# Moving eight record scatters of GpSimd from the attention phase into the first dense steps

## The chip, the cores and the metric

The program runs on one core of a Trainium2 chip. The metric is the time of one execution on the device in microseconds (us). The engines are TensorE (PE; PEld is its weight load), VectorE (DVE), ScalarE (ACT), GpSimd (POOL) and SyncE (SP), which here only issues transfers.

## The reference

Sigmoid attention is followed by a mixture of experts in which each token goes to one expert.

```python
# q, k, v: [8 batches, 12 heads, 448 tokens, 64]
scores = q @ k.T / sqrt(64) - log(448)
attn_out = sigmoid(scores) @ v
x = attn_out.transpose(0, 2, 1, 3).reshape(3584, 768)
logits = x @ w_gate                       # [3584, 8]
expert_idx = argmax(logits, axis=1)
gate_w = softmax(logits)[arange, expert_idx]
for e in range(8):
    mask = expert_idx == e
    out[mask] = gate_w[mask, None] * (relu(x[mask] @ w1[e]) @ w2[e])   # w1[e]: 768x1024, w2[e]: 1024x768
```

## The kernel before

**Two parts in one stream.** The whole order is written by hand. `attention()` is a generator over steps s. A step is one chunk of 64 keys for two pairs of heads: `scores` (L616), sigmoid on ScalarE (L602), `weighted` (L632). There are 168 such steps, 21 for each batch (`PB`). Below step `START` = 70 the steps hold attention alone, two steps at a time. From step 70 on (the dense part), TensorE mostly runs expert matmuls: the caller runs seven of them each time that `attention()` yields (`MIX` is (7, 7), so fourteen a step), and every seventh step holds a burst of seven attention steps.

**The dense expert work.** `moe(b, wts)` runs the 448 tokens of one batch through one expert, the one that most of that batch's tokens chose. A w1 block j (eight for a batch) is 18 matmuls (L240) into one of two PSUM buffers (`ps`), then a relu on ScalarE that gives the high part `hh` (L247), and a VectorE operation that gives the low part `hl` (L248) and frees the PSUM buffer. Then come three output blocks d of twice 24 matmuls (L263) with w2.

**Weights in two parts.** A weight tile is loaded by SyncE's queue into `wst` (five buffers), split by ScalarE into a high part (L159) and by GpSimd, which subtracts the high part from the raw tile, into a low part (L160): a w1 part is 128x768, a w2 part 128x512. `Weights.ahead(n)` issues these splits. A w1 block calls it at its start with 3, 4, 5, 6, 7, 9, 11 and 13 parts for blocks 0 to 7 (the first eight parts are w1, then twelve w2); in an output block it is called after every second group of three matmuls of the second half, for one part more each time. The first three w1 parts are split before step 70.

**Where each token goes.** After attention for a batch b, stages named by letters are issued at fixed steps: "b", "c", "c2", "c3" work out the choice of expert and the gates, "d" (`gate_d`) ends by writing `si`, the four columns of slot indices of that batch (L403), a tile with two buffers. Stages "s0" to "s3" (`gate_d2`) write the batch's records (token number and gate, eight bytes) into the list `recs` in DRAM, one column of 112 tokens at a time, with an indirect transfer on GpSimd's queue (L424). "s0" first fills the token numbers on GpSimd (L413) and copies the gates on VectorE (L416). Nothing reads `recs` before the dense part is over; then the tokens that didn't go to their batch's expert are gathered by it.

**What sets the order around the change.** `PLACES` maps a step to its stages. A place r of batch b stands at step (b + 1) * 21 + r; below step 70 an odd one is moved up by one. So the first batch's scatters stand at steps 34, 36, 38 and 40, the second's at 56, 58, 60 and 62. In the dense part a step's stages stand between its two groups of seven matmuls. "d" of batch 2 stands at step 78. During attention's own phase GpSimd's queue also issues K loads (L545) and V loads (L558, L562) of the first 22 pairs; in the dense part those are on SyncE's queue.

Of the kernel before, what the change touches and what calls it, by code (L numbers as in the profile page):

```python
# [24 lines left out]
def tile_sigmoid_attention_top1_moe(  # L25
# [632 lines left out]
    START = 70  # L658
# [3 lines left out]
    PB = NP // 2 * ST  # L662
# [10 lines left out]
    def attention():  # L673
# [53 lines left out]

        LATE = {8: "b", 10: "c", 11: ("l", "c2"), 12: "c3", 15: "d", 16: "g", 26: "e"}
        FOUR = ("s0", "s1", "s2", "s3")
        PUTS = 2 * (dict(zip((13, 15, 17, 19), FOUR)),) + 4 * (dict(zip((27, 28, 29, 30), FOUR)),)  # L730
        PUTS += (dict(zip((25, 26, 27, 28), FOUR)), {9: "s0", 10: "s1"})
        LAST = {3: "b", 5: "c", 6: ("l", "c2"), 7: "c3", 8: "d", 9: "g"}
        EARLY = {5: "b", 7: ("c", "c2"), 9: ("l", "c3"), 11: "d", 13: "g", 32: "e"}
# [2 lines left out]
        for b in range(B):  # L736
            places = (EARLY, EARLY, FIRST_LATE, LATE, LATE, LATE, LATE, LAST)[b]
            for r, what in [*places.items(), *PUTS[b].items()]:
                at = (b + 1) * PB + r
# [20 lines left out]
        for s in range(N_ST + 11):  # L760
# [19 lines left out]
            if s >= START:  # L780
                b, r = divmod(s - 3 * PB, PB)
# [35 lines left out]
    for s, n in attention():  # L817
        if s >= START:
            more(n)
# [362 lines left out]
```

## Time and profile before

| | us |
|---|---|
| median of 3 runs (lowest to highest) | 776.97 (776.0 to 777.6) |
| the profiled execution, own time | 776.84 |
| its span, first to last instruction | 775.0 |
| TensorE matmul busy | 768.4 |
| TensorE weight load busy | 593.3 |
| VectorE busy | 373.9 |
| ScalarE busy | 384.1 |
| GpSimd busy | 349.6 |

The granted clock of TensorE is 1.000 over the span. Busy times are unions of what ran on an engine; the end of a matmul is modelled, so the start times of matmuls tell more than their ends. In rows of a timeline the columns are the start and the duration in us, engine, line, operation, output<-inputs, shapes and count; what stands in brackets is the idle time of the engine before it and what ended it.

### The profile page before, as it was taken

How to read it: one execution, taken by the hardware profiler on the slowest of the kernel's cores; microseconds unless marked ns; L12 is line 12 of the kernel's file. 1: busy time of each engine (PE TensorE's matmuls, PEld its weight loads, DVE VectorE, ACT ScalarE, POOL GpSimd, SP SyncE). 2: the span in 40 equal slices, each digit the busy share in tenths (PEclk: the TensorE clock that was granted, in tenths of full speed). 3: DMA queues.
4: the chain of work that ended last, by engine and by line, in shares of the span. 5: the costliest groups of instructions: out<-in, count | busy, mean ns of one | idle time of the engine just before them, and what ended most of it. 6: DMA issues, size and time to landing. Idle time of an engine off the chain costs nothing. (4 is left out here: it accounts for less than half of the span.)

```text
span 775.0 us, 15532 instructions
## 1 busy us (share of the span) xinstructions
PE 768.4 (99%) x5586; PEld 593.3 (77%) x5586; DVE 373.9 (48%) x806; ACT 384.1 (50%) x688; POOL 349.6 (45%) x330
## 2 busy tenths in 40 slices
PE   9999999999999999999999999999999999999997
PEld 6555557687696786867868769677698999999996
DVE  2354584465264652537426384254736493244543
ACT  5877776645536455264443653545523342444451
POOL 8648554242352342531615316054265764664351
PEclk9999999999999999999999999999999999999999
DMA  9777798976758846587585876766167554655770
GB/s 207 169 160 157 171 251 197 210 171 154 169 129 173 201 107 166 139 190 168 116 194 84 193 169 144 183 168 166 38 171 170 157 146 118 202 143 155 220 223 38
DMA packets 311633, 125.67 MB, mean 162 GB/s; under 512 B 210062, under 2 KB 307006, under 8 KB 311552
## 3 DMA queue, kind: packets, MB, share of 16 engines
q1 hardware_dynamic: 305504, 112.42, 61.9%
q0 software_dynamic: 5760, 11.76, 5.4%
q8 instruction: 45, 0.74, 0.4%
q10 hardware_dynamic: 288, 0.46, 0.2%
q14 instruction: 36, 0.29, 0.1%
HBM read 102.49 MB, written 22.49 MB: 161 GB/s over the span
## 5 line engine op out<-in xcount | busy, mean ns | idle before, releaser
L602 ACT ACTIVATE at<-sc,bias_s 128x448 f32<-128x448 f32 x336 | 192.3, 633 | 107.4 <-PE sc L616 106.5
L160 POOL TENSOR_TENSOR w1l<-wst,w1h 128x768 fp32r<-128x768 f32 x72 | 132.7, 1853 | 173.9 <-ACT w1h L159 172.2
L160 POOL TENSOR_TENSOR w2l<-wst,w2h 128x512 fp32r<-128x512 f32 x84 | 107.0, 1298 | 138.7 <-ACT w2h L159 121.0
L616 PE MATMUL sc<-qt,kt 64*64 64x448 f32 x1344 | 167.3, 545 | 0.0
L632 PE MATMUL av<-at,vn 64*64 64x448 f32 x1344 | 165.0, 536 | 0.0
L240 PE MATMUL ps<-xh,w1h 128*128 128x448 f32 x336 | 124.4, 370 | 0.2 <-DVE nw L439 0.2
L240 PE MATMUL ps<-xh,w1l 128*128 128x448 f32 x336 | 123.4, 367 | 0.0
L240 PE MATMUL ps<-xl,w1h 128*128 128x448 f32 x336 | 123.3, 367 | 0.0
L263 PE MATMUL ps<-hh,w2l 128*128 128x448 f32 x336 | 123.3, 367 | 0.0
L263 PE MATMUL ps<-hl,w2h 128*128 128x448 f32 x336 | 123.2, 367 | 0.0
L263 PE MATMUL ps<-hh,w2h 128*128 128x448 f32 x336 | 122.7, 365 | 0.0
L616 PEld LDWEIGHTS sc<-qt,kt 64*64 64x64 f32 x1344 | 78.2, 189 | 56.9 <-issue 44.4
L632 PEld LDWEIGHTS av<-at,vn 64*64 64x64 f32 x1344 | 59.4, 133 | 64.3 <-issue 53.5
L159 ACT CAST w2h<-wst 128x512 fp32r<-128x512 f32 x108 | 64.7, 620 | 75.7 <-PE ps L263 64.5
L247 ACT ACTIVATE hh<-ps 128x448 fp32r<-128x448 f32 x56 | 30.6, 546 | 139.6 <-PE ps L240 137.0
L276 DVE TENSOR_TENSOR ps<-ps,gt 128x448 f32<-128x448 f32 x42 | 40.7, 969 | 85.4 <-PE ps L263 85.3
L495 DVE STREAM_TRANSPOSE xt<-av 128x448 f32<-128x448 f32 x46 | 27.3, 629 | 101.5 <-PE av L632 100.4
L248 DVE SCALAR_TENSOR_TENSOR hl<-ps,hh 128x448 fp32r<-128x448 f32 x56 | 34.4, 614 | 78.3 <-ACT hh L247 76.8
L240 PEld LDWEIGHTS ps<-xh,w1h 128*128 128x128 f32 x336 | 63.1, 188 | 9.9 <-issue 4.4
L263 PEld LDWEIGHTS ps<-hh,w2l 128*128 128x128 f32 x336 | 65.2, 194 | 6.6 <-issue 3.5
L263 PEld LDWEIGHTS ps<-hl,w2h 128*128 128x128 f32 x336 | 65.2, 194 | 6.2 <-issue 3.2
L263 PEld LDWEIGHTS ps<-hh,w2h 128*128 128x128 f32 x336 | 65.2, 194 | 3.4 <-DVE nw L439 0.2
(158 smaller groups left out, 918.9 us busy)
## 6 DMA issues: line engine op xcount, KB each, us to landing
wst<-in_moe_w_dram SPq DMA_DIRECT2D x72, 384.0 KB, 3.3
wst<-in_moe_w_dram SPq DMA_DIRECT2D x54, 512.0 KB, 5.1
x_tok<-xt SPq DMA_DIRECT2D x64, 168.0 KB, 2.8
qn<-in_q_dram SPq DMA_DIRECT2D x184, 56.0 KB, 3.1
raw<-x_tok SPq DMA_DIRECT2D x28, 336.0 KB, 6.2
out_dram<-ob SPq DMA_DIRECT2D x84, 112.0 KB, 2.4
kn<-in_k_dram SPq DMA_DIRECT2D x104, 56.0 KB, 3.3
kn<-in_k_dram POOLq DMA_DIRECT2D x80, 56.0 KB, 4.0
```

What stands on the lines that cost most here:

```text
L159: nc.scalar.copy(hi, st)
L160: eng.tensor_tensor(lo, st, hi.bitcast(F32), op=ALU.subtract)
L240: nc.tensor.matmul(ps[:, :S], a[:, ws], b_, start=(t == 0 and n == 0), stop=(t == KD - 1 and n == 2))
L247: nc.scalar.activation(hh[:, :S], ps[:, :S], AF.Relu)
L248: nc.vector.scalar_tensor_tensor(hl[:, :S], ps[:, :S], 0.0, hh[:, :S].bitcast(F32), op0=ALU.max, op1=ALU.subtract)
L263: nc.tensor.matmul(ps[:, :S], a, b_, start=(j == 0 and n == 0), stop=(j == KF - 1 and n == 2))
L276: nc.vector.tensor_tensor(by_gate, by_gate, gate_rows[b], op=ALU.mult)
L495: nc.vector.transpose(xts[b][:, :, t, :], pv[:, :S].rearrange("p (j s) -> p j s", s=32))
L602: nc.scalar.activation(at, ps[:, :S], AF.Sigmoid, bias=bias_s, scale=SCALE)
L616: nc.tensor.matmul(ps[quarter(g, h), :S], ks, ops[g, "q"][OWN[h]], start=True, stop=True)
L632: nc.tensor.matmul(psv[g][OWN[h], :S], ops[g, "v"][rows, c, :], at[rows], start=(c == 0), stop=(c == KC - 1))
```

## The change

Only the places of the scatters of the first two batches differ. The new tuple gives the first batch the steps 70, 72, 74 and 76 (`START - PB` is 49, and 21 is added back), the second the steps 80, 82, 84 and 86. The fills and copies of "s0" move with them. The other six batches keep their places. The number of instructions is the same.

```diff
         FOUR = ("s0", "s1", "s2", "s3")
-        PUTS = 2 * (dict(zip((13, 15, 17, 19), FOUR)),) + 4 * (dict(zip((27, 28, 29, 30), FOUR)),)
+        PUTS = tuple(dict(zip(range(r, r + 8, 2), FOUR)) for r in (START - PB, START + 10 - 2 * PB)) + 4 * (dict(zip((27, 28, 29, 30), FOUR)),)
         PUTS += (dict(zip((25, 26, 27, 28), FOUR)), {9: "s0", 10: "s1"})
```

## Rows read from the trace of the kernel before

**Rows 1.** The page's first part: busy us (share of span) and count.

```profile
PE 768.4 (99%) x5586; PEld 593.3 (77%) x5586; DVE 373.9 (48%) x806; ACT 384.1 (50%) x688; POOL 349.6 (45%) x330
```

**Rows 2.** TensorE's waits, whole span: us in total, times, longest.

```profile
PE ps L240 <- DVE nw L439: 0.2, 1, 0.2
```

**Rows 3.** Timeline of TensorE in attention's own phase.

```profile
14.56 1.66 PE L616 MATMUL sc<-qt,kt 64*64 64x448 f32 x12
...
29.59 1.66 PE L616 MATMUL sc<-qt,kt 64*64 64x448 f32 x12
...
61.71 2.02 PE L632 MATMUL av<-at,vn 64*64 64x448 f32 x16
...
73.73 2.02 PE L632 MATMUL av<-at,vn 64*64 64x448 f32 x16
```

**Rows 4.** Line 424, all 32 scatters: duration in ns, who waited, landing.

```profile
L424 POOL DMA_INDIRECT recs<-rec,si x32: 941/958/1045, 63.0 to 609.6; - x32
...
  POOL kn L545: 0.4, 1
...
DMA to landing us min/median/max: 2.6/3.2/7.5
```

**Rows 5.** Timeline of GpSimd in attention's own phase: a scatter.

```profile
111.47 0.96 POOL L424 DMA_INDIRECT recs<-rec,si  x1 [0.30 <-issue]
```

**Rows 6.** Timeline of GpSimd, 131 to 198 us.

```profile
131.09 1.84 POOL L160 TENSOR_TENSOR w1l<-wst,w1h 128x768 fp32r<-128x768 f32 x1 [5.13 <-ACT w1h L159]
...
158.94 1.29 POOL L160 TENSOR_TENSOR w2l<-wst,w2h 128x512 fp32r<-128x512 f32 x1
160.63 2.56 POOL L160 TENSOR_TENSOR w2l<-wst,w2h 128x512 fp32r<-128x512 f32 x2 [0.40 <-ACT w2h L159]
164.48 2.55 POOL L160 TENSOR_TENSOR w2l<-wst,w2h 128x512 fp32r<-128x512 f32 x2 [1.28 <-ACT w2h L159]
184.61 5.06 POOL L160 TENSOR_TENSOR w2l<-wst,w2h 128x512 fp32r<-128x512 f32 x4 [17.58 <-DMA x_tok<-xt]
194.37 3.80 POOL L160 TENSOR_TENSOR w2l<-wst,w2h 128x512 fp32r<-128x512 f32 x3 [4.70 <-ACT w2h L159]
```

**Rows 7.** Timeline of VectorE, 163 to 165 us.

```profile
163.72 0.17 DVE L403 TENSOR_SCALAR si<-sl 112x4 uint32<-112x4 f32 x1
163.90 0.65 DVE L570 STREAM_TRANSPOSE qt<-qn 128x448 f32<-128x448 f32 x1
164.47 0.58 DVE L248 SCALAR_TENSOR_TENSOR hl<-ps,hh 128x448 fp32r<-128x448 f32 x1
```

**Rows 8.** All waits: GpSimd's w1 subtractions for ScalarE.

```profile
POOL w1l L160 <- ACT w1h L159: 172.2, 44, 15.4
```

**Rows 9.** Timeline of TensorE, around 166.8 and 191.6 us.

```profile
166.79 0.37 PE L263 MATMUL ps<-hh,w2h 128*128 128x448 f32 x1
...
191.58 0.36 PE L263 MATMUL ps<-hh,w2l 128*128 128x448 f32 x1
```

**Rows 10.** Waits of SyncE's queue: weight loads for GpSimd's w2 subtractions.

```profile
SPq L183 <- POOL w2l L160: 45.3, 19, 8.6
```

**Rows 11.** Timeline of GpSimd, 593 to 596 us.

```profile
593.35 1.85 POOL L160 TENSOR_TENSOR w1l<-wst,w1h 128x768 fp32r<-128x768 f32 x1 [0.92 <-ACT w1h L159]
```

**Rows 12.** Timeline of VectorE, 593 to 596 us.

```profile
593.75 1.47 DVE L403 TENSOR_SCALAR si<-sl 112x4 uint32<-112x4 f32 x1
595.14 0.61 DVE L248 SCALAR_TENSOR_TENSOR hl<-ps,hh 128x448 fp32r<-128x448 f32 x1
```

**Rows 13.** Timeline of TensorE, 595 to 597 us.

```profile
595.80 0.47 PE L240 MATMUL ps<-xh,w1h 128*128 128x448 f32 x1 [0.19 <-DVE nw L439]
```

**Rows 14.** Line 424 from 412 to 414 us: the scatter at 413, its landing.

```profile
DMA to landing us min/median/max: 7.5/7.5/7.5
```

**Rows 15.** Two windows: busy us (count) by engine, granted clock, DMA share, GB/s.

```profile
160.00:165.00 5.00, 5.00 (x28) 4.43 (x27) 3.62 (x14) 2.65 (x6) 3.31 (x4) 1.00 0.93 255
415.00:420.00 5.00, 5.00 (x27) 4.46 (x26) 3.92 (x10) 1.51 (x4) 4.53 (x4) 1.00 0.95 167
```

## The prediction

> **What bounds the kernel now.** I read the page's busy times first, then the waits of TensorE, then TensorE's timeline where the eight scatters now stand, and last the queues around the places they go to. TensorE is busy for 768.4 of 775.0 us [rows 1]; busy time alone proves little, as matmul ends are modelled, so the waits decide: in the whole span, beyond the first microseconds, TensorE is shown waiting once, for 0.2 us [rows 2]. In attention's own phase a block of sixteen attention matmuls starts every 1.50 us: ten blocks from 14.56 to 29.59, where no scatter runs, take 15.03 us, and eight from 61.71 to 73.73, through which the first batch's four scatters are issued, take 12.02 us [rows 3]. The cadence is the same with and without them. So the program is a chain of TensorE work with no holes; a change elsewhere pays only if it opens a hole, and can save almost nothing.
>
> **What is removed from attention's phase.** Eight scatters, two index fills (an iota each) and two copies of gates into the records. A scatter keeps GpSimd 0.96 us in the median, 0.94 to 1.05 [rows 4], after 0.30 us of issue [rows 5], so 1.26 us each and 10.1 us for eight. What stands behind a scatter on that queue are loads of K and V, and one such load waited 0.4 us for a scatter, the only instruction that is shown waiting for one [rows 4]. Since TensorE's cadence does not know of the scatters, the gain is taken as 0. Its bounds: 0 below, 0.4 us above.
>
> **Where they go.** GpSimd does not follow the steps by itself; it runs through its list and is held by ScalarE, which makes the high part before GpSimd can subtract the low one. So each scatter's time comes from its place between subtractions. A dense step issues seven expert matmuls, then the stages, then seven more; a w1 block has 18 matmuls and calls for its weights ahead at its start.
>
> First batch. The scatter of step 70 follows the third w1 subtraction, which ended 5.13 us before the fourth began at 131.09 [rows 6]; iota, copy (a 112x4 operation on VectorE is 0.17 us [rows 7]) and scatter fit in that idle time. Those of steps 72 and 74 follow the fourth and the sixth subtraction, where GpSimd also waits for ScalarE's next high part; it does so 44 times ahead of a w1 subtraction, 3.9 us on average [rows 8], three times a scatter. Each of these costs 0. The scatter of step 76 is different: seven matmuls, numbers 84 to 90, are issued first, and number 90 opens the sixth w1 block, which calls for the eighth w1 part and the first w2 part. So it lands behind the w2 subtraction at 158.94 and ahead of the pair at 160.63 [rows 6]. It would start at 158.94 + 1.29 + 0.30 = 160.53 and end at 161.49; the pair starts 0.86 us late and ends at 164.05 instead of 163.19.
>
> Second batch. The scatter of step 80 stands behind the w2 pair of 164.48, which ends at 167.03, and ahead of an idle time of 17.58 us [rows 6]: cost 0. That of step 82 falls between the first and second of the four subtractions from 184.61, which run back to back at 1.265 us [rows 6]. The last three move by 1.26 us. The third of the four (the tile of w1 blocks 6 and 7 for the second output block) ends at 188.4 and is first read at 191.58 [rows 6, 9]: 3.2 us of cover, of which 1.9 are left. That of step 84 stands in the 4.70 us of idle time before 194.37, that of step 86 between the second and third of the three there [rows 6]; that third part is for the last output block of the batch and is read later than the two before it. Cost on TensorE: 0; each microsecond beyond the cover would cost one. Raw weight tiles are released up to 1.26 us later, and SyncE's queue, with loads of K, Q and V and stores behind each weight load, waits for that release: it already waits there 19 times, up to 8.6 us [rows 10], and TensorE shows nothing of it, so 0 again.
>
> **The step that is not free.** Two things meet on VectorE at 163.72, where batch 2 writes its slot indices si [rows 7]. First, si has two buffers, so batch 2 overwrites batch 0's: the write now has to wait until the scatter of step 76 has landed, where before that scatter was over in attention's phase. Second, VectorE's small operations can be held by a GpSimd subtraction until that ends: at 593.75 the same line took 1.47 us instead of 0.17 and ended with the subtraction that ran from 593.35 to 595.20 [rows 11, 12]. Behind si on VectorE stand a Q transpose and then hl of w1 block 6, which frees the PSUM buffer that the first w2 matmul takes at 166.79 [rows 9]; hl now ends at 164.47 + 0.58 = 165.05 [rows 7], with 1.74 us to spare. At 593.75 that cover was used up: hl ended at 595.75, and TensorE stood 0.19 us before its matmul at 595.80 [rows 12, 13].
>
> With the pair moved, the additions and the sum just before si are held until 164.05 by the second subtraction; two more small operations, of some 0.2 us each as si itself [rows 7], bring si to about 164.5, just when the next subtraction begins (164.48 [rows 6]), so it is held to 165.75. Transpose (0.57 us by the starts at 163.90 and 164.47 [rows 7]) and hl (0.58 us) then end at 166.9 to 167.0, and TensorE starts 0.1 to 0.2 us late. Bounds: 0, if si slips in ahead of that subtraction, and 0.4 us, if the start adds as much again as the 0.19 us before 595.80 [rows 13]. I take 0.2 us. The landing does not change that while it comes by 165.75, 5.2 us after the issue; the median of the landings shown is 3.2 us [rows 4].
>
> The sum: 776.84 us (own time of the profiled execution: span 775.0 and 1.8 around it) - 0 + 0 + 0.2 = 777.04. The median of the runs shown is 776.97, 0.13 above that execution, so the forecast on the median's footing is 777.2 us.
>
> **Two rules against the rows.** Rows: every one of 32 scatters took 0.94 to 1.05 us [rows 4], 24 of them in the dense part beside VectorE's work. The Trainium skill (SBUF — State Buffer, section "SBUF: two separate sides", the box on "DVE blocks DMA") says that GpSimd cannot write descriptors while VectorE runs an operation in a two-port mode, and gives 3100 ns in place of 620. By its factor of five, an estimate, the scatter of step 82 would take 4.8 us and the sum would be 779.1; no row of this trace shows it. For the landing, rows show 2.6 to 7.5 us from issue. The skill's fixed cost of about 2 us for a transfer on this path (DMA: Bandwidth & Descriptors, "Anatomy of one DMA — SWDGE (gpsimd) path") would have step 76's scatter landed, by estimate, at 161.5 + 2.0 = 163.5, without any wait; the rows run longer.
>
> **The rivals.**
> A. Slower: the landing is late, and batch 2's si waits for it. The landing of 7.5 us belongs to the scatter at 413 us [rows 14], after which the DMA engines were 0.95 busy; from 160 to 165 they are 0.93 busy [rows 15]. With 7.5 us si is written at 168.0, hl ends at 168.0 + 0.17 + 0.57 + 0.58 = 169.3, and TensorE loses 2.5 us: 779.5. It decides from a landing of 5.2 us on; at 6.7 us the loss passes 1.5 us. Against it: the median of 3.2.
> B. Faster: attention's phase gains. GpSimd has 10.1 us more there, but the one wait to be saved is 0.4 us [rows 4]: 776.6, which no measurement tells from no change. To be more, a hole must exist that the cadence [rows 3] denies.
> C. Slower: VectorE holds up a scatter, as GpSimd held VectorE's si by 1.30 us [rows 7, 12]. It decides for the scatter of step 82 from a hold of 1.9 us on, and every microsecond beyond is one of TensorE's; three holds of 1.30 us in a row would cost 3.9 - 1.9 = 2.0 us: 779.2. Against it: no scatter took over 1.05 us [rows 4].
>
> **How the numbers follow.** About 0.2% (1.6 us) is what a measurement can tell from no change here. Forecast (0 to 0.4 us, or a landing a little late): 0.70. A with its loss past 1.5 us: 0.19. B beyond what the rows show: 0.07. C: 0.04. So faster 0.07, within 0.2% 0.70, slower 0.23. The runs shown spread from 776.0 to 777.6; the likeliest case has 776.0 to 778.0, and the range, which takes in A to its full price, is 775.9 to 779.6.
>
> **What would show it.** In the new profile: attention's blocks at 1.50 us with only loads on GpSimd; four scatters each at about 126 to 161 and 168 to 198, near 0.97 us; the w2 pair of 160.63 at about 161.5; si of batch 2 ending near 165.8 rather than 163.9, and the first w2 matmul at 166.8 to 167.0. A is right if si ends near 168 and TensorE starts w2 near 169. The prediction is wrong if TensorE waits anywhere else by over a microsecond, or if the attention blocks run faster than 1.50 us.

## The result, and the profile after

The changed kernel takes 781.19 us (median of 6 runs, 780.63 to 781.99) beside 776.98 us for the kernel before (6 runs, 776.0 to 777.6): ratio 1.0055, interval 1.0043 to 1.0067. It is slower by 4.2 us, outside the range of 775.9 to 779.6. The profiled execution took 781.52 us of its own time, with a span of 779.7 us.

TensorE's waits in the changed kernel (us in total, times, longest), where [rows 2] had one of 0.2 us:

```profile
PE ps L263 <- DVE nw L439: 2.1, 1, 2.1
PE sc L616 <- DVE logits L295: 1.7, 1, 1.7
...
PE ps L240 <- DVE nw L439: 0.2, 1, 0.2
```

Two holes are new, and nothing else; the page's busy line has 0.7 us more of TensorE than [rows 1], so the loss is waiting, not work:

```profile
PE 769.1 (99%) x5586; PEld 593.6 (76%) x5586; DVE 380.3 (49%) x806; ACT 384.6 (49%) x688; POOL 348.7 (45%) x330
```

TensorE's timeline after says where they are:

```profile
61.55 2.02 PE L632 MATMUL av<-at,vn 64*64 64x448 f32 x16
...
73.58 1.67 PE L632 MATMUL av<-at,vn 64*64 64x448 f32 x14
...
116.94 1.78 PE L616 MATMUL sc<-qt,kt 64*64 64x448 f32 x12
...
120.38 0.65 PE L616 MATMUL sc<-qt,kt 64*64 64x448 f32 x2 [1.66 <-DVE logits L295]
...
171.24 0.48 PE L263 MATMUL ps<-hh,w2h 128*128 128x448 f32 x1 [2.09 <-DVE nw L439]
```

The eight blocks from 61.55 to 73.58 take 12.03 us, as in [rows 3]. The first hole stands at 118 to 120 us, just before the phase ends. By the GpSimd subtraction of [rows 6] that moves from 158.94 to 161.14, it costs 2.2 us. The second stands before the first w2 matmul: 166.79 [rows 9] has become 171.24, 4.45 us later, so 2.25 us come on top. Together they are 4.45 of the 4.7 us by which the profiled spans differ. One was never on my list; the other is rival A.

**The first hole, read backwards.** TensorE waits for the PSUM buffer that VectorE's copy of the logits (L295) frees. These are VectorE's rows before, then after:

```profile
104.10 0.60 DVE L477 STREAM_TRANSPOSE whole<-raw 128x448 f32<-128x448 f32 x1
...
116.08 0.63 DVE L481 TENSOR_TENSOR xl<-whole,xh 128x448 fp32r<-128x448 f32 x1
...
117.19 0.35 DVE L295 COPY logits<-psg 128x224 f32<-128x224 f32 x1
```

```profile
105.38 0.65 DVE L477 STREAM_TRANSPOSE whole<-raw 128x448 f32<-128x448 f32 x1 [1.36 <-DMA raw<-x_tok]
...
117.34 2.16 DVE L481 TENSOR_TENSOR xl<-whole,xh 128x448 fp32r<-128x448 f32 x1
...
119.98 0.34 DVE L295 COPY logits<-psg 128x224 f32<-128x224 f32 x1
```

The split of batch 0's tokens (`whole`, `xh`, `xl`) begins 1.28 us late, because the load of the raw token tile lands late. The split's last operation then takes 2.16 us in place of 0.63, and the logits come 2.79 us later. GpSimd's rows show what changed there, before and after:

```profile
94.38 0.16 POOL L413 IOTA rec<- 112x4 uint32 x1
100.20 1.01 POOL L424 DMA_INDIRECT recs<-rec,si  x1 [5.66 <-issue]
101.21 2.56 POOL L545 DMA_DIRECT2D kn<-in_k_dram  x4
...
116.94 1.83 POOL L160 TENSOR_TENSOR w1l<-wst,w1h 128x768 fp32r<-128x768 f32 x1 [3.83 <-ACT w1h L159]
```

```profile
94.22 2.55 POOL L545 DMA_DIRECT2D kn<-in_k_dram  x4
...
117.20 1.81 POOL L160 TENSOR_TENSOR w1l<-wst,w1h 128x768 fp32r<-128x768 f32 x1 [4.29 <-ACT w1h L159]
```

Before, the second batch's first scatter stood 5.66 us at the head of the queue, and with it stood four K loads. They left at 101.21. What the scatter waited for is VectorE's copy of the gates into its records, which ends at 99.37, behind the write of its indices; the queue's own wait is the longest of line 424 in the kernel before (6168 ns):

```profile
99.21 0.16 DVE L416 COPY rec<-gates 112x4 f32<-112x4 f32 x1
```

```profile
L424 POOLq EVENT_SEMAPHORE  x8: 17/17/6168, 59.2 to 596.4; - x8
```

Without the scatter the K loads leave at 94.22, beside the token load, which SyncE issues at about 94 us in both kernels. So the scatter had been a brake. That early K loads make the token load late is tested below; how they do it, by sharing the DMA engines, is argued and not shown. The subtraction that splits the first weights ran from 116.94 before, just after `xl` had ended (116.71). Now VectorE is late, and `xl` starts at 117.34, inside the subtraction (117.20 to 119.01), and ends at 119.50, after it.

**The second hole** is the predicted place. GpSimd's and VectorE's rows after:

```profile
161.14 1.29 POOL L160 TENSOR_TENSOR w2l<-wst,w2h 128x512 fp32r<-128x512 f32 x1
162.59 0.95 POOL L424 DMA_INDIRECT recs<-rec,si  x1 [0.15 <-issue]
163.55 2.54 POOL L160 TENSOR_TENSOR w2l<-wst,w2h 128x512 fp32r<-128x512 f32 x2
```

```profile
164.82 1.34 DVE L398 TENSOR_TENSOR rk<-rk,region 112x32 f32<-112x32 f32 x1
...
169.83 0.17 DVE L403 TENSOR_SCALAR si<-sl 112x4 uint32<-112x4 f32 x1 [3.23 <-DMA recs<-rec,si]
170.04 0.65 DVE L570 STREAM_TRANSPOSE qt<-qn 128x448 f32<-128x448 f32 x1
170.60 0.58 DVE L248 SCALAR_TENSOR_TENSOR hl<-ps,hh 128x448 fp32r<-128x448 f32 x1
```

The scatter of step 76 was issued at 162.59 and landed 7.2 us later; `si` of the third batch waited 3.23 us for it, and the transpose and `hl` stood behind `si`. TensorE starts at 171.24, just after `hl` ends at 171.18; the profile puts the wait down to `nw` (L439), the small operation behind `hl`. All 32 scatters, by line 424:

```profile
L424 POOL DMA_INDIRECT recs<-rec,si x32: 939/948/1045, 129.0 to 612.6; - x32
...
  DVE si L403: 3.2, 1
...
DMA to landing us min/median/max: 2.4/3.8/8.3
```

### The profile page after: what moved, and what is told of

Its sections match the earlier page's. It is cut to its first block, busy times and chain, and to the rows that moved or that the text cites. A ratio compares the mean times of both kernels' runs of the same rounds, so it can differ in the third digit from the quotient of the medians.

```text
span 779.7 us, 15544 instructions
## 1 busy us (share of the span) xinstructions
PE 769.1 (99%) x5586; PEld 593.6 (76%) x5586; DVE 380.3 (49%) x806; ACT 384.6 (49%) x688; POOL 348.7 (45%) x330
## 3 DMA queue, kind: packets, MB, share of 16 engines
q1 hardware_dynamic: 305504, 112.42, 61.0%
## 5 line engine op out<-in xcount | busy, mean ns | idle before, releaser
L616 PE MATMUL sc<-qt,kt 64*64 64x448 f32 x1344 | 169.6, 545 | 1.7 <-DVE logits L295 1.7
```

The source lines that it names most:

```text
L616: nc.tensor.matmul(ps[quarter(g, h), :S], ks, ops[g, "q"][OWN[h]], start=True, stop=True)
```

## The experiments

Each kernel was timed beside the kernel before on the same chip, and the ratio is to that. The kernel before had 777.43 us in the first session (the first four kernels) and 777.43 in the second (the next four), 776.39 in the third (the next three), 776.89 in the fourth.

**1. Each batch alone.** Only the first batch's scatters moved (`x1_first_only`, the first diff), or only the second's (`x2_second_only`, the second):

```diff
-        PUTS = 2 * (dict(zip((13, 15, 17, 19), FOUR)),) + 4 * (dict(zip((27, 28, 29, 30), FOUR)),)
+        PUTS = (dict(zip((49, 51, 53, 55), FOUR)), dict(zip((13, 15, 17, 19), FOUR))) + 4 * (dict(zip((27, 28, 29, 30), FOUR)),)
```

```diff
-        PUTS = 2 * (dict(zip((13, 15, 17, 19), FOUR)),) + 4 * (dict(zip((27, 28, 29, 30), FOUR)),)
+        PUTS = (dict(zip((13, 15, 17, 19), FOUR)), dict(zip((38, 40, 42, 44), FOUR))) + 4 * (dict(zip((27, 28, 29, 30), FOUR)),)
```

> Only the first batch's scatters are moved; the second batch's stay in attention's phase. Theory of two holes: the second batch's first scatter again holds the four K loads behind it from 94 to 101 us, the token load is in time and TensorE has no hole at 118; the hole ahead of the first w2 matmul (2.3 us, si waiting for the landing of the scatter of step 76) stays. Time 2.0 to 2.5 us above before: 779.0 to 779.5. Rival (the scatters' own GpSimd time in the dense part is what costs, four of eight): also about 2.2 us above, but spread over small waits for low parts, with no wait of 2 us for si.

Measured: 777.64 us, ratio 1.0002 (0.9993 to 1.0011). No hole at all: the first went as expected, the second did not come. The K loads stay held (at 100.87), the scatter of step 76 (160.31) stays, and it lands late, but nothing waits for it. Its landing, and VectorE's rows at that place:

```profile
DMA to landing us min/median/max: 6.4/6.4/6.4
```

```profile
164.36 1.28 DVE L403 TENSOR_SCALAR si<-sl 112x4 uint32<-112x4 f32 x1
165.55 0.63 DVE L570 STREAM_TRANSPOSE qt<-qn 128x448 f32<-128x448 f32 x1
166.12 0.58 DVE L248 SCALAR_TENSOR_TENSOR hl<-ps,hh 128x448 fp32r<-128x448 f32 x1
```

`si` ends at 165.64, a microsecond before that scatter lands. The likely reason is that the third batch's `si` was given the buffer of the second batch, whose scatters stayed early; the trace doesn't name the buffers, so this is not shown. I had not foreseen it. The miss is useful: it shows `si` held by a GpSimd subtraction alone (1.28 us in place of 0.17 [rows 7]). `hl` ends at 166.70, the first w2 matmul starts at 166.75 (166.79 [rows 9]), and TensorE shows no wait: the hold uses up the cover and no more.

> Only the second batch's scatters are moved. Theory of two holes: the K loads go out at 94 us beside the token load, VectorE is late by 1.3 us, is held once more by the first w1 subtraction, and TensorE has the hole at 118 (2.2 us); si is written at once and there is no hole ahead of the first w2 matmul. Time 2.0 to 2.5 us above before: 779.0 to 779.5. Rival (own GpSimd time): the same sum, but no hole at 118, since nothing is added there.

Measured: 779.34 us, ratio 1.0024 (1.0014 to 1.0034), with the first hole alone, 1.7 us as TensorE's wait:

```profile
PE sc L616 <- DVE logits L295: 1.7, 1, 1.7
```

**2. A brake removed, and nothing put into the dense part** (`x5_later_in_attention`). The kernel before, with the second batch's scatters one pair of steps later:

```diff
-        PUTS = 2 * (dict(zip((13, 15, 17, 19), FOUR)),) + 4 * (dict(zip((27, 28, 29, 30), FOUR)),)
+        PUTS = (dict(zip((13, 15, 17, 19), FOUR)), dict(zip((15, 17, 19, 21), FOUR))) + 4 * (dict(zip((27, 28, 29, 30), FOUR)),)
```

> The kernel before, with nothing moved into the dense part: only the second batch's four scatters stand one pair of steps later (steps 58 to 64 in place of 56 to 62), so that the K loads of step 56 no longer stand behind a held scatter. Theory (those loads then go out at 94 us beside the token load, which lands late and delays VectorE's last gate operations): TensorE's hole at 118 to 120 us appears, 2.0 to 2.5 us, and the time is 779.0 to 779.6 us. Rival (the loss comes from work added to the dense part or taken out of attention): no hole, 776.6 to 777.6.

Measured: 779.56 us, ratio 1.0032 (1.0020 to 1.0045). GpSimd's and VectorE's rows repeat the pattern of the changed kernel, with all eight scatters still in attention's phase:

```profile
93.80 2.55 POOL L545 DMA_DIRECT2D kn<-in_k_dram  x4
```

```profile
104.92 0.65 DVE L477 STREAM_TRANSPOSE whole<-raw 128x448 f32<-128x448 f32 x1 [1.25 <-DMA raw<-x_tok]
...
117.29 2.15 DVE L481 TENSOR_TENSOR xl<-whole,xh 128x448 fp32r<-128x448 f32 x1
```

So the first hole has nothing to do with the dense part; it comes from the first scatter's leaving its place ahead of the K loads.

**3. The subtraction out of the way** (`x6_weights_later`). The changed kernel, with the first w1 parts split later:

```diff
-    FIRST = (START - 5, START - 3, START - 1)
+    FIRST = (START - 3, START - 2, START - 1)
```

> The changed kernel with the first three w1 parts split at steps 67, 68 and 69 in place of 65, 67 and 69. Theory: the hole at 118 us has two parts, the late token tile (about 0.7 us of it) and the first GpSimd subtraction, which holds VectorE's last token operation for 2.16 us in place of 0.63 (1.5 us of it). Without the second part the hole is 0.5 to 0.9 us, the other hole at 167 us stays 2.2 to 2.5, and the time is 779.4 to 780.0. Rival 1 (the late token tile alone makes the hole): it stays at 2 us, 781.0 to 781.6. Rival 2 (the later parts are late for the first dense steps): a new wait of TensorE near 121 us for the low parts, 1 us or more, 780.5 or more.

Measured: 778.40 us (777.05 to 780.3), ratio 1.0017 (1.0007 to 1.0027); its profiled execution took 777.35 us. A miss twice, to the better side. The first hole is gone entirely, though the token tile is as late as ever (1.16 us of wait at 104.49):

```profile
116.45 0.62 DVE L481 TENSOR_TENSOR xl<-whole,xh 128x448 fp32r<-128x448 f32 x1
116.99 0.64 DVE L570 STREAM_TRANSPOSE kt<-kn 128x448 f32<-128x448 f32 x1
117.55 0.35 DVE L295 COPY logits<-psg 128x224 f32<-128x224 f32 x1
```

The late tile alone is absorbed; together with the subtraction it is not. And the second hole is gone too, with the wait of `si` for the scatter still in the program: here that scatter landed in 2.1 us. The windows show what differs; first the changed kernel, then this one (the last two columns are the DMA share and GB/s):

```profile
160.00:166.00 6.00, 6.00 (x32) 5.34 (x32) 2.63 (x8) 2.10 (x5) 5.83 (x5) 1.00 0.95 251
```

```profile
160.00:166.00 6.00, 6.00 (x32) 5.31 (x31) 4.75 (x12) 2.42 (x5) 5.33 (x6) 1.00 0.52 124
```

In the changed kernel SyncE issued four token stores from 158.87 and two weight loads of 512 KB from 161.12, just ahead of the scatter (162.59). Here the scatter (160.22) came ahead of the stores (160.97) and of the loads (164.52). That the order of issue made the landing short is argued from these rows. Only the profiled execution shows this; the median lies 1.05 us above that execution, so other executions may have lost something there, which stays open.

**4. The second hole's cause, with two buffers** (`x8_close_hold_gone`). The changed kernel, with the first batch at steps 70 to 73:

```diff
-        PUTS = tuple(dict(zip(range(r, r + 8, 2), FOUR)) for r in (START - PB, START + 10 - 2 * PB)) + 4 * (dict(zip((27, 28, 29, 30), FOUR)),)
+        PUTS = tuple(dict(zip(r, FOUR)) for r in ((49, 50, 51, 52), range(START + 10 - 2 * PB, START + 18 - 2 * PB, 2))) + 4 * (dict(zip((27, 28, 29, 30), FOUR)),)
```

> The changed kernel with the first batch's scatters at steps 70 to 73 in place of 70, 72, 74 and 76, and nothing else: all eight scatters in the dense part, two buffers for the slot indices. Theory: the hole at 167 us goes, because the last of the four has landed long before the third batch's slot indices are written at 164 us; the one at 118 us stays at 2.0 to 2.6; 778.8 to 779.5. Rival (the hole at 167 us comes from the scatters' load on GpSimd and the transfer engines there, not from the wait for the landing): 780.8 to 781.6, or half of it.

Measured: 779.40 us, ratio 1.0029 (1.0018 to 1.0040). The second hole is gone, the first stays (1.5 us as TensorE's wait). The same four scatters, still in the dense part, open no second hole when the last is issued at 139.09. This kernel also takes the scatter away from between the w2 subtractions, and with it their hold of `si` (0.17 us again), so it doesn't tell the landing from that hold; `x12_ten_si` in 6 does.

**5. Both cured.** `x7_close_together` puts the first batch at steps 70 to 73, leaves the second batch's first scatter at step 56 as the brake, and its other three at 82, 84 and 86, where the changed kernel has them (the expectation says 80, 82 and 84; by the diff it is these):

```diff
-        PUTS = tuple(dict(zip(range(r, r + 8, 2), FOUR)) for r in (START - PB, START + 10 - 2 * PB)) + 4 * (dict(zip((27, 28, 29, 30), FOUR)),)
+        PUTS = (dict(zip((49, 50, 51, 52), FOUR)), {13: "s0", 40: "s1", 42: "s2", 44: "s3"}) + 4 * (dict(zip((27, 28, 29, 30), FOUR)),)
```

> The changed kernel, two buffers for the slot indices as before, with the first batch's scatters at steps 70 to 73 (one apart) and the second batch's first one left at step 56; its other three at steps 80, 82 and 84. Seven scatters are still moved into the dense part. Theory: the K loads stay held and the scatter of step 73 has landed by 155 us, before the third batch's slot indices are written; neither hole, 776.8 to 777.6. Rival (each scatter in the dense part costs GpSimd's own time, about 0.5 us): 780.5 to 781.0.

Measured: 776.71 us, ratio 0.9991 (0.9982 to 1.0000), and no hole. `x9_both_mended` moves all eight and takes the edits of 3 and 4 together:

> The changed kernel with both cures at once: the first three w1 parts split at steps 67, 68 and 69, and the first batch's scatters at steps 70 to 73. All eight scatters stay in the dense part. Theory (the two holes are two separate waits, each with its own cure, and the scatters themselves cost TensorE nothing there): no hole, 776.6 to 777.5. Rival (a rest of GpSimd's own time stays): 778.0 or more, without a hole in the profile.

Measured: 777.08 us, ratio 1.0010 (1.0001 to 1.0020), and no hole. So without the two holes the change was measured at -0.7 us (seven scatters moved) and +0.7 us (all eight). It gives nothing: neither version beats the kernel before by what can be measured.

**6. More buffers for the slot indices.** My first test of the second hole gave `si` a third buffer: in the changed kernel (`x3_three_si`), and with the second batch's first scatter left at step 56 as well (`x4_hold_kept`).

```diff
-        si = small.tile([GP, NCH], U32, tag="si", bufs=2, name=f"si_{b}")
+        si = small.tile([GP, NCH], U32, tag="si", bufs=3, name=f"si_{b}")
```

> The changed kernel with three buffers for si in place of two, so that batch 2's si waits for no scatter. Theory (landing): the hole ahead of the first w2 matmul shrinks from 2.3 us to at most 0.4; the one at 118 stays: 778.9 to 779.5. Rival (the moved w2 subtractions hold VectorE, not the landing): the hole stays at about 2 us, 781.2. Rival (own GpSimd time): 781.2.

Measured: 783.64 us, ratio 1.0090 (1.0065 to 1.0114). The second hole is gone, but a new one stands near 490 us, where an output store lands late:

```profile
PE sc L616 <- DVE logits L295: 4.3, 2, 2.6
```

```profile
493.35 0.65 DVE L277 STREAM_TRANSPOSE ob<-ps 128x448 f32<-128x448 f32 x1 [7.01 <-DMA out_dram<-ob]
```

> The changed kernel with three buffers for si, and with the second batch's first scatter (its fill, its copy and its transfer) left at step 56; the other seven scatters stay in the dense part. Theory of two holes: the K loads are held back again, the token load is in time, both holes are gone: 776.6 to 777.4, as before. Rival (own GpSimd time): seven scatters still cost some 3.7 us: 780.7.

Measured: 779.88 us, ratio 1.0031 (1.0017 to 1.0045), with no hole in the profile, and yet 2.45 us above the kernel before. What the two share is in the rows of the DMA queues (packets, MB, share of the 16 engines), first the kernel before, then `x3_three_si`:

```profile
q1 hardware_dynamic: 305504, 112.42, 61.9%
q0 software_dynamic: 5760, 11.76, 5.4%
```

```profile
q1 hardware_dynamic: 305504, 112.42, 66.4%
q0 software_dynamic: 5760, 11.76, 6.7%
```

The same packets and bytes, and more time. By the tile sizes in the kernel, with a slot of 32 bytes per partition for each buffer of `si`, a third buffer shifts every tile behind it in the on-chip memory by 32 bytes; the tiles of K, Q, V and the stored tokens lie there, in the kernel before at multiples of 256. The traces hold no addresses, so this layout is a reckoning, and only its effects were measured. Three kernels changed only the count: `x11_before_three_si` in the kernel before, `x10_four_si` (64 bytes) and `x12_ten_si` (256 bytes) in the changed one.

> The kernel before with three buffers for the slot indices in place of two, no scatter moved. Theory (the 32 bytes by which the tiles behind them shift make the transfers of K, Q, V and the tokens longer): the hardware queue's share rises from 62 to about 66%, four token stores take about 2.5 us of issue in place of 2.06, and the time is 778.5 to 780.5, with little of it in waits of TensorE that the profile names. Rival (the third buffer does harm only where scatters were moved): share 62%, 776.6 to 777.5.

Measured: 778.72 us, ratio 1.0028 (1.0018 to 1.0038), with no scatter moved:

```profile
q1 hardware_dynamic: 305504, 112.42, 65.6%
```

`x4_hold_kept` lost about as much, 2.45 us. Transfers of tiles behind `si` land later: the token stores in 3.3 us in place of 2.8, and the K loads of GpSimd's queue as the rows below say, before and then here (KB each, median us to landing). The output stores, whose tiles stand ahead of `si` by the same reckoning, land in 2.4 us in both.

```profile
kn<-in_k_dram POOLq DMA_DIRECT2D x80, 56.0 KB, 4.0
```

```profile
kn<-in_k_dram POOLq DMA_DIRECT2D x80, 56.0 KB, 5.3
```

> The changed kernel with four buffers for the slot indices in place of two; nothing else. The tiles behind them in the on-chip memory shift by 64 bytes per partition, where three buffers shifted them by 32. Theory: the hole at 167 us goes and the one at 118 us stays, as with three buffers, but the transfers run at the share of the changed kernel (the hardware queue at 61 to 62%, not 66%) and no late store follows near 490 us: 778.8 to 779.6. Rival (the third buffer's loss came from the freed waits themselves, not from the addresses): the hole at 490 us and the share of 66% come again, 782 to 784.

Measured: 780.30 us, ratio 1.0053 (1.0039 to 1.0067). The second hole is gone, but the share is 64.9%: my guess that 64 bytes would do fell.

```profile
q1 hardware_dynamic: 305504, 112.42, 64.9%
```

> The changed kernel with ten buffers for the slot indices, so that no write of them waits for a scatter and the tiles behind them shift by 256 bytes per partition. Theory (shifts of 32 and 64 bytes slow the transfers by where their tiles then lie, and 256 bytes put the tiles on the same footing as two buffers do): the hardware queue's share is 61 to 62% again, the hole at 167 us is gone, the one at 118 us stays, no drift after it; the time is 2.0 to 2.7 us above the kernel before. Rival (any other number of buffers than two slows the transfers, or freed waits do): a share of 65% or more and 3.5 us or more above the kernel before.

Measured: 778.88 us, ratio 1.0029 (1.0018 to 1.0041), 1.99 us above the kernel before, with the first hole alone:

```profile
q1 hardware_dynamic: 305504, 112.42, 61.3%
```

This is the clean form of the test that `x3_three_si` spoiled. The scatter of step 76 keeps its place (162.42), and `si`, held by a subtraction, takes 1.28 us; only the wait for the landing is gone, and the second hole with it. Why a store came so late near 490 us in that one kernel was not isolated; that it goes with the longer transfers is argued, not shown.

**All together** (us above the kernel before of the same session, and TensorE's holes in the profiled execution; x3 has a third, near 490):

| kernel | median | ratio | us | hole at 118 | hole at 167 |
|---|---|---|---|---|---|
| changed | 781.19 | 1.0055 | +4.2 | yes | yes |
| x2, second batch alone | 779.34 | 1.0024 | +1.9 | yes | no |
| x5, one pair later in attention | 779.56 | 1.0032 | +2.1 | yes | no |
| x8, first batch at 70 to 73 | 779.40 | 1.0029 | +2.0 | yes | no |
| x12, ten buffers | 778.88 | 1.0029 | +2.0 | yes | no |
| x6, weights later | 778.40 | 1.0017 | +1.0 | no | no |
| x1, first batch alone | 777.64 | 1.0002 | +0.2 | no | no |
| x7, both cured, brake kept | 776.71 | 0.9991 | -0.7 | no | no |
| x9, both cured, all eight moved | 777.08 | 1.0010 | +0.7 | no | no |
| x11, before with three buffers | 778.72 | 1.0028 | +2.3 | no | no |
| x4, three buffers, brake kept | 779.88 | 1.0031 | +2.5 | no | no |
| x10, four buffers | 780.30 | 1.0053 | +3.9 | yes | no |
| x3, three buffers | 783.64 | 1.0090 | +6.2 | yes | no |

Four kernels that have the first hole alone, and no slower transfers, lie 1.9 to 2.1 us above the kernel before. Of the 4.2 us, then, 2.1 to 2.3 belong to the second hole, as its 2.25 us in the profile said.

## Why the prediction was wrong, step by step

- **What is removed from attention's phase: the step that failed.** I priced it at 0, with bounds of 0 and 0.4 us of gain, because "TensorE's cadence does not know of the scatters" [rows 3]. The cadence is indeed unchanged. But that asks only whether the scatters delay TensorE, not what they delay to its advantage. I took 0.30 us of issue from the scatter at 111.47 [rows 5] for all; the one at 100.20 stood 5.66 us, with four K loads behind it. The profile books such a stand as "issue", so the wait of 0.4 us in [rows 4] did not show it; the scatter's own row and the queue's wait of 6168 ns did. Taking it from there cost 1.9 to 2.1 us (x2, x5, x8, x12), a loss where the bounds allowed only a gain.
- **That hole needs two things at once.** Without the early K loads (x1, x7) it is absent; with them and a later subtraction (x6, x9) it is absent too. The Trainium skill (SBUF — State Buffer, "Who interferes with whom") says that a VectorE instruction with two inputs in on-chip memory contends with a GpSimd instruction that reads there, and that the later one is blocked until the earlier has ended. The trace agrees: `xl` took 2.16 us, begun inside a subtraction, and 0.62 to 0.63 outside one. Four later ones (L483) that began inside a subtraction took 1.03 to 1.45 us in place of 0.58.
- **The first three scatters of the first batch, and all four of the second, cost 0: right.** They took 0.94 to 1.05 us, and no hole stands near them; with both cures, eight scatters in the dense part cost nothing that shows as a wait (x9). Rival C fell with that. Its mechanism does exist: in x5 two scatters, still in attention's phase, took 1.40 and 1.39 us, each begun 0.05 to 0.06 us after an `xl` subtraction of VectorE (0.62 to 0.63 us). That is some 0.45 us a time, a third of what C had taken, and no moved scatter met it. The Trainium skill's rule on descriptors written beside VectorE (SBUF — State Buffer, "SBUF: two separate sides") gives 3100 ns in place of 620 for a transfer beside a VectorE copy in a two-port mode; no scatter here grew by such a factor, but no row says whether an operation in that mode ran beside one.
- **Step 76: place right.** Taking off the 2.20 us of the first hole, its scatter began at 160.39 (160.53 predicted) and the pair at 161.35 (161.5).
- **si and hl: the mechanism was rival A's, at its price.** The hold by the subtraction alone was rightly sized: in x1 `si` took 1.28 us and TensorE shows no wait for it. The landing was mis-sized: I went by the median of 3.2 us and gave A 0.19, though [rows 14, 15] held a landing of 7.5 us, and a DMA share of 0.93 just where this scatter would land. It took 7.2 us; A's price was 2.5 us, the hole is 2.25. (A's own sum also has a loss of 1.5 us from a landing of 6.4 us on, not 6.7.) x8 and x12 take the wait away, and the hole goes; x12 leaves all else in place. x6 shows the other side: the same scatter, beside a share of 0.52, landed in 2.1 us.
- **The range.** It reached to A's full price alone. Either hole alone would have left the time inside (the first alone, x2: 779.34; the second alone, by its 2.25 us and not run, some 779.2); both together put it outside.
- **SyncE's queue: 0 was right** for TensorE: no wait for weights appears.
- **Rival B**, the gain, did not come: the best version, x7, is 0.9991 (0.9982 to 1.0000). That attention's phase gains nothing was right.

Three things stay open: how the early K loads delay the token load, the 0.7 us by which x9 stands above the kernel before, with no wait in its profile, and the 1.05 us by which x6's median exceeds its profiled execution.

## What to carry to other kernels

Before an instruction is taken out of a queue that runs in order, look at what stands behind it and since when: an idle time booked as "issue" may be a brake that other transfers profit from. Price a wait for a transfer by the landings in stretches with the same DMA share, not by the median over the span. When a buffer is added as a test, pad it so that the tiles behind it keep their alignment, and compare the queues' shares before believing the time.

## What was not expected of the hardware

- **Where a tile lies changes what its transfers cost.** The same 305504 packets and 112.42 MB took 61.0 to 62.2% of the engines' span in the ten kernels whose tiles, by the reckoning above, keep to multiples of 256 bytes, and 64.9 to 66.8% in the four where they are shifted by 32 or 64 bytes. In the kernel before, the shift of 32 alone cost 2.3 us, with no wait of TensorE that the profile names. Shifts of 128 bytes were not tried. The Trainium skill (DMA: Bandwidth & Descriptors, "How a descriptor splits into AXI transactions") says that a transaction has to start at a multiple of 256 bytes, and that a descriptor that starts elsewhere pays for bytes it does not use. The runs go the same way as that rule, in the time of the transfers; they show no transactions.
- **A landing depends on what was issued just ahead.** One and the same scatter landed in 7.2 and 6.4 us (the changed kernel, x1), with four stores and at least one weight load of 512 KB issued just ahead of it; in 4.4 us (x3), with the stores ahead and the loads behind; and in 2.1 us (x6, x10), with both behind. That the order is the reason is argued from these five.
